# Two feature tiles of the first token chunk side by side, and a last output tile in two halves

## Chip, core and metric

The kernel runs on one core of a Trainium2 chip. The metric is the device time of one launch in microseconds; beside it stands a profile of one execution. TensorE (PE) multiplies, VectorE (DVE) and ScalarE (ACT) move data out of PSUM and split it, GpSimd (POOL) fills constants, and SyncE (SP) issues most DMAs; some stores of the last stage are issued from ScalarE's queue.

## What is computed

Two independent results stand side by side in the output, 2048 x 896 in float32:

```python
def _A_ref(x, dft_seq_re, dft_seq_im, dft_hid_re, dft_hid_im):
    a = jnp.einsum("bsd,ed->bse", x, dft_hid_re)
    b = jnp.einsum("bsd,ed->bse", x, dft_hid_im)
    y = jnp.einsum("ts,bse->bte", dft_seq_re, a) - jnp.einsum("ts,bse->bte", dft_seq_im, b)
    return y

def _B_ref(x, wqkv, wo):
    B, S, D = x.shape          # 1, 2048, 448
    H = 16; Dh = D // H
    qkv = (lambda x, *d: x.transpose(*d))((x @ wqkv).reshape(B, S, 3, H, Dh), 2, 0, 3, 1, 4)
    q, k, v = qkv[0], qkv[1], qkv[2]
    scores = jnp.einsum("bhqd,bhkd->bhqk", q, k) * Dh ** -0.5
    p = _softmax(scores, axis=-1)
    o = jnp.einsum("bhqk,bhkd->bhqd", p, v)
    return (lambda x, *d: x.transpose(*d))(o, 0, 2, 1, 3).reshape(B, S, D) @ wo
```

A is a Fourier mixing of hidden and sequence axis, B attention with 16 heads of 28.

## The kernel before

The tokens of B are cut into four chunks of 512 (`CH`), the columns of query and key weights into seven tiles of 128 (j), the token rows into 16 tiles of 128. Every float32 operand is split into a high part (a copy to fp32r, mostly by ScalarE) and a low part (source less high part, by VectorE); a product is then eleven matmuls (`products`: three k-tiles with high-high, low-high and high-low, and two for the 64 rows that are left). The program has these stages:

- `load_x` loads a chunk of x in four pieces (L573), converts each (L575) and subtracts (L481). `Piece` (by `weights_of`) loads one weight tile (L606), converts it into `whi` (L607) and subtracts it into `wlo` (L611, L620). `load_w` does the same for the value weights, which lie in the tile `wd` (L590, L591, and L481 by the helper `sub`).
- `project(j, w, chunks)` makes tile j of queries and keys for some chunks, eleven matmuls each (L636, by `chain`), copies the bank out (L485 or L487), subtracts the low part (L678) and stores both in DRAM (L681, L682). `values` does the value products (L636 again, with `wd` as the moving operand) and copies them with L711.
- `tops` bounds the scores' maximum from the first keys (matmul L1418, transposition L1421), and its row goes through DRAM (`md`, L1427, L1470) into the query tile.
- `head_once` makes scores (L1434), their exponentials on ScalarE (L1438), and products with the values (L1445) in groups of 16 score tiles. Matmuls of the other stages fill the gaps: first the rest of the projections, then the hidden-axis stage of A (L891), then its sequence-axis stage (L1175), then the output projection (`project_late`: L1669 for three k-tiles, L1700 for the last one).

The order of instructions isn't written by hand. Every operation is a task of `Schedule` with a key (about when it is due), an estimated duration, the tasks that it waits for and the buffers that it takes; a list scheduler walks through time, gives each free engine the ready task of the lowest key, and emits it. So one edit can move instructions on every engine far behind it. On each engine and in each queue what was emitted runs in order. PSUM has eight banks: `fill_s` holds 0 to 3 (all stages but scores), `bank_s` 4 to 7, and it may borrow. `kept` is a pool of 20 buffers of 128 x 2 x 512.

`chain` keeps its matmuls in order among themselves and with all other chains by a shared list:

```python
    last = [None]
...
        last[0] = pe(key + i * d, emit, d=d, deps=[last[0], *more], use=[*use, o, *(then if i == n - 1 else ())])
```

At the start the program warms TensorE with products of the identity (L1528), and asks for chunk 0 of x, the weights of tile 0, the value weights and the other chunks, in this order. In the last stage tiles 8 to 15 of the output have nine of their eleven matmuls in a bank (L1669), the last two are added (L1700), the bank is copied out, and the tile (128 x 448) is stored: odd tiles from ScalarE's queue (L1710), even ones from SP's (L1712). A flag is read by all engines at the end (L1742); it decides on a second way through the program that isn't taken here.

Of the kernel before, what the change touches and what calls it, by code (L numbers as in the profile page):

```python
# [14 lines left out]
AF = mybir.ActivationFunctionType  # L15
# [7 lines left out]
D = 448  # L23
H = 16
DH = 28
P = 128
NT = S // P
CH = 512
NC = S // CH
# [12 lines left out]
QT = NT // NQ  # L42
Q_YO = 2
N_WARM = 11
VALUES = (4, 4, 4, 4)
LEAD = 30.0
LIMIT = 1e36
# [292 lines left out]
def tile_kernel(ctx, tc, xa, wre, wim, wd, xb, wqkv, wo, out):  # L340
# [118 lines left out]
    def pe(key, emit, n=1, d=MS, lat=0.25, **kw):  # L459
        return sch.add({"PE": n * d}, key, emit, lat=lat, **kw)  # L460
# [185 lines left out]
    v_done = {}  # L646
    x_users = []

    def project(j, w, chunks):

        for c in chunks:
            cols = slice(c * CH, (c + 1) * CH)
            o = fill_s.slot()
            xh, xl, x3 = lambda k, cols=cols: lz(x_h, k, cols), lambda k, cols=cols: lz(x_l, k, cols), lambda cols=cols: lz(x_3, cols)
            wh, wl = lambda k: (lambda: w.hi.t[:, k]), lambda k: (lambda: w.lo.t[:, k])
            first = j == 0
            seq = [(b, a) for a, b in products(xh, xl, x3, wh, wl)]
            if first and c == 0:

# [11 lines left out]
            pair = None if st else kept_s.slot()  # L671
            hi, lo = (stage_s.slot(), stage_s.slot()) if st else (Half(pair, 0), Half(pair, 1))
            own = [hi, lo] if st else [pair]
            end = chain(key, seq, o, CH, [], [w.hi, w.lo], M512, own, parts)
            key, out_key = (0.0, 11.0) if first else (key - 10, key - 10)
            as_r, as_f = (lambda t, st=st: t if st else f32r(t)), (lambda t, st=st: f32(t) if st else t)
            a = sch.add({"ACT": ACT_P, "DVE": DVE_P}, key, lambda e, o=o, hi=hi: copy_of(e, as_r(hi.t), o.t), deps=[end], use=[o, *own])
            b = dve(key, lambda o=o, hi=hi, lo=lo: nc.vector.tensor_tensor(  # L678
# [5 lines left out]

    def weights_of(j):
        key = fkey(0, 0) - 12
        return Piece(lambda: wqkv[:, :, j * P:(j + 1) * P], 0.2 if j == 0 else key, "w", j == 0)

    def values(ready, chunks):
        HH = H // 2  # L690
# [837 lines left out]
            nc.tensor.matmul(o.t[:, :P], ident, ident, start=True, stop=True)  # L1528
    pe(-1.0, warm, n=N_WARM, d=0.43, acq=[o])
    load_x(0, 0.1)  # L1530
    w_0 = weights_of(0)
    wv = load_w(w_first, lambda k: wqkv[:, k, 2 * D:], 1.5, early=True)
    for c in range(1, NC):
        load_x(c, 1.0 + 3 * c)
    project(0, w_0, [0])
    values(wv, [0])
    project(0, w_0, [1, 2, 3])
    values(wv, [1, 2, 3])
    x_users.append(v_last[0])
    for j in range(1, 7):  # L1540
        project(j, weights_of(j), range(NC))
    key = fkey(0, 0)
    staged = [d for j in range(1, 5) for c in range(NC) for d in qk_done[j, c]]
    ready = weights_both(key - 11, [v_last[0], *staged])
# [86 lines left out]
    def project_late(w, w_ready):  # L1631
# [29 lines left out]
        for n in range(NT):  # L1661
# [5 lines left out]
            for i, (a, b) in enumerate(seq):  # L1667
                def emit(e, i=i, a=a, b=b, o=o, n=n):
                    nc.tensor.matmul(o.t[:, :D], a(), b(), start=(i == 0), stop=(i == 8 and n < N_HELD))  # L1669
# [23 lines left out]
        for n in range(NT):  # L1693
            c, t = divmod(n, 4)
            key = T_OUT + n
            o = bank_s.slot() if n < N_HELD else held[n][0]

            def emit(e, n=n, o=o, xt=x3[c], t=t):
                for i, y in enumerate((w.h, w.l)):
                    nc.tensor.matmul(o.t[:, :D], xt.t[:, t * P:(t + 1) * P], y[:, 3], start=(i == 0 and n < N_HELD), stop=(i == 1))  # L1700
            p = pe(key, emit, n=2, d=M448, deps=[x3_ready[c], *w_ready, *([] if n < N_HELD else [held[n][1]])], use=[o, x3[c]])
            if n < N_HELD:
                s, at, put = held[n]
                e = dve(key, lambda o=o, at=at: nc.vector.tensor_tensor(at(), at(), o.t[:, :D], op=ALU.add), 0.53, deps=[p, put], use=[o, s])
                dma(key, lambda at=at, n=n: nc.sync.dma_start(out[n * P:(n + 1) * P, D:], at()), deps=[e], use=[s])
            else:
                pair = kept_s.slot()
                e = sch.add({"ACT": 0.43, "DVE": 0.53}, key, lambda e, o=o, pair=pair: copy_of(e, pair.t[:, 0, :D], o.t[:, :D]), deps=[p], use=[o, pair])
                if n % 2:
                    dma_act(key, lambda pair=pair, n=n: nc.scalar.dma_start(out[n * P:(n + 1) * P, D:], pair.t[:, 0, :D]), 3.0, deps=[e], use=[pair])  # L1710
                else:
                    dma(key, lambda pair=pair, n=n: nc.sync.dma_start(out[n * P:(n + 1) * P, D:], pair.t[:, 0, :D]), deps=[e], use=[pair])  # L1712
# [91 lines left out]
```

## Time and profile before

| | us |
|---|---|
| median of three runs | 798.05 |
| lowest and highest of them | 796.93, 800.04 |
| time of the profiled execution | 799.37 |
| its span, first to last instruction | 797.6 |
| TensorE busy in it | 785.1 (98%) |
| ScalarE busy | 598.9 (75%) |
| VectorE busy | 434.4 (54%) |

Times of the trace count from the start of the span. The profiled execution took 1.8 us more than its span, and 1.3 us more than the median. A busy TensorE isn't TensorE at its peak, since a matmul's modelled end lies behind the next one's start; how fast matmuls follow each other is read from their starts. Mean granted clock over the span: 0.994.

### The profile page before, as it was taken

Reading aid. Unit: us, or ns where it says so; the run is one execution under the profiler, and the core shown is the slowest. Engines: PE = TensorE matmul, PEld = TensorE weight load, DVE = VectorE, ACT = ScalarE, POOL = GpSimd, SP = SyncE. Lnnn points to the kernel's source line nnn. Section 1 sums busy time; section 2 is a strip of 40 time slices with the busy share of each in tenths; the row PEclk is TensorE's granted clock in tenths of the full one; section 3 lists DMA queues with packets and bytes.
Section 4 is the critical chain, followed back from the end, with each engine's and each line's share of the span. In section 5 each row is a group of like instructions: output and inputs, shape, how many; then the busy total and the mean of one; then the engine's idle time right before and its main releaser. Section 6 shows DMA issues by size and latency. Waiting matters only on the chain.

```text
span 797.6 us, 14127 instructions
## 1 busy us (share of the span) xinstructions
PE 785.1 (98%) x4721; PEld 476.4 (60%) x4721; DVE 434.4 (54%) x914; ACT 598.9 (75%) x1243; POOL 51.7 (6%) x201
## 2 busy tenths in 40 slices
PE   8999999999999999999999999999999999999997
PEld 7886556576666555555555555555545555555586
DVE  6641443363244363523455986466966968485850
ACT  6106877558778778888888888888888978888941
POOL 3000000000000000000002111011201201101000
PEclk9999999999999999999999999999989999999999
DMA  9657866452584554546459775649848768775642
GB/s 299 213 174 245 222 200 210 135 188 85 155 170 144 165 179 144 152 151 203 131 158 312 240 222 158 219 144 265 264 112 239 231 203 257 254 223 155 184 149 96
DMA packets 138610, 152.58 MB, mean 191 GB/s; under 512 B 31140, under 2 KB 109538, under 8 KB 138530
## 3 DMA queue, kind: packets, MB, share of 16 engines
q1 hardware_dynamic: 137954, 150.69, 61.7%
q8 instruction: 39, 0.64, 0.3%
q10 hardware_dynamic: 576, 0.92, 0.3%
q14 instruction: 41, 0.34, 0.1%
HBM read 110.39 MB, written 50.86 MB: 202 GB/s over the span
## 4 chain that ended last, share of the span: by engine, by line
PE 88%; issue 5%; SPq 2%; DMA 2%; DVE 1%; ACT 1%; POOL 0%; DVEq 0%; POOLq 0%
PE bank L1434 31%; PE bank L1445 27%; PE bank L636 11%; PE bank L1175 10%; PE bank L891 4%; PE bank L1669 4%; PE bank L1700 1%; ACT kept L1438 1%; DMA kept<-wqkv 1%; DMA abd<-kept 1%; PE bank L1418 1%; SPq L1296 1%; PE bank L1518 0%; PE bank L1094 0%; SPq L1297 0%
## 5 line engine op out<-in xcount | busy, mean ns | idle before, releaser
L1438 ACT ACTIVATE kept<-bank 128x512 f32<-128x512 f32 x1024 | 509.8, 669 | 140.6 <-PE bank L1434 135.0
L1434 PE MATMUL bank<-q,k 85*128 85x512 f32 x1024 | 364.1, 424 | 3.3 <-DVE kept L1421 1.3
L1434 PEld LDWEIGHTS bank<-q,k 85*128 85x128 f32 x1024 | 184.3, 190 | 97.2 <-issue 27.4
L1445 PE MATMUL bank<-kept,v 128*32 128x512 f32 x2048 | 234.0, 597 | 0.0
L1445 PEld LDWEIGHTS bank<-kept,v 128*32 128x32 f32 x2048 | 60.1, 110 | 133.8 <-issue 130.3
L1175 PE MATMUL bank<-zt 128*128 128x226 bf16 x448 | 75.1, 265 | 0.0
L487 DVE COPY kept<-bank 128x226 f32<-128x226 f32 (+3 forms) x58 | 27.7, 499 | 81.1 <-PE bank L891 46.8
L636 PE MATMUL bank<-xt,whi 128*128 128x512 f32 x196 | 69.2, 399 | 1.1 <-DVE xt L481 1.1
L1175 PEld LDWEIGHTS <-zt 128*128 128x128 bf16 x448 | 31.0, 99 | 31.0 <-issue 20.6
L636 PEld LDWEIGHTS bank<-xt,whi 128*128 128x128 f32 x196 | 36.7, 190 | 13.2 <-issue 2.5
L1218 DVE TENSOR_TENSOR zt<-wdraw,xraw 128x508 bf16<-128x508 f32 x28 | 19.1, 682 | 45.7 <-PE bank L1175 30.3
L1131 DVE TENSOR_REDUCE diff<-zt 128x1 f32<-128x512 bf16 x66 | 43.5, 672 | 0.9
L636 PE MATMUL bank<-xt,wlo 128*128 128x512 f32 x112 | 43.8, 393 | 0.0
L891 PE MATMUL bank<-wd,whi 128*128 128x450 f32 (+3 forms) x128 | 43.1, 376 | 0.0
L1175 PE MATMUL bank<-xt,whi 128*128 128x448 f32 (+1 forms) x128 | 39.4, 337 | 0.0
L636 PE MATMUL bank<-wd,xt 128*128 128x448 f32 x176 | 37.8, 369 | 0.6 <-DVE wd L481 0.6
L636 PEld LDWEIGHTS bank<-wd,xt 128*128 128x128 f32 x176 | 32.7, 188 | 4.7 <-issue 1.0
L1129 ACT ACTIVATE spent<-zt 128x512 uint8<-128x512 bf16 x46 | 31.6, 686 | 4.0 <-DVE zt L1213 1.9
L485 ACT ACTIVATE kept<-bank 128x448 f32<-128x448 f32 (+5 forms) x21 | 11.7, 588 | 26.4 <-PE bank L1700 13.0
L487 DVE CAST wd<-bank 128x512 fp32r<-128x512 f32 x11 | 7.6, 691 | 40.3 <-PE bank L636 36.9
L1224 POOL TENSOR_TENSOR zt<-wdraw,xraw 128x2 bf16<-128x2 f32 x28 | 9.1, 325 | 302.1 <-DMA wdraw<-wre 143.8
L1421 DVE STREAM_TRANSPOSE kept<-bank 128x512 f32<-128x512 f32 (+1 forms) x20 | 14.2, 711 | 26.0 <-PE bank L1418 25.9
(171 smaller groups left out, 756.4 us busy)
## 6 DMA issues: line engine op xcount, KB each, us to landing
wdraw<-wim SPq DMA_DIRECT2D x38, 256.0 KB
qkd<-wd SPq DMA_DIRECT2D x32, 256.0 KB
wdraw<-wre SPq DMA_DIRECT2D x32, 256.0 KB
q<-qkd SPq DMA_DIRECT2D x64, 112.0 KB
k<-qkd SPq DMA_DIRECT2D x64, 112.0 KB
abd<-kept SPq DMA_DIRECT2D x16, 448.0 KB
kept<-abd SPq DMA_DIRECT2D x16, 448.0 KB
qkd<-kept SPq DMA_DIRECT2D x24, 256.0 KB
```

The costliest lines, as they stand in the source:

```text
L487: nc.vector.tensor_copy(dst, src)
L636: nc.tensor.matmul(o.t[:, :cols], w(), x(), start=(i == 0), stop=(i == n - 1))
L891: nc.tensor.matmul(o.t[:, c0:c1], of(w, i), y(), start=n == 0, stop=n == m)
L1129: nc.scalar.activation(spent, src(), AF.Abs, accum_out=dst)
L1131: nc.vector.tensor_reduce(dst, src(), axis=AX.X, op=ALU.add, apply_absolute_value=True)
L1175: nc.tensor.matmul(o.t[:, at0:at0 + n], cut_of(w.t, e, c), x(), start=first, stop=stop)
L1218: e.tensor_tensor(turned(dl.t, 1, 1, P - 1), mirror(r.t), read(base.t, 1, 1, P - 1), op=minus)
L1421: r = dve(key, lambda o=o, mt=mt: nc.vector.transpose(mt.t[:32 * n, 0], o.t[:32 * n]), 0.64, deps=[m], acq=[mt], use=[o], own=RAW_S)
L1434: m = pe(key, lambda e: nc.tensor.matmul(b.t, KT[h][kt // 4].t[:KR + 1, kt % 4 * P:(kt % 4 + 1) * P], q.t[:KR + 1, :], start=True, stop=True),
L1438: return act(key - 20, lambda: nc.scalar.activation(p.t, b.t, AF.Exp, scale=SCALE), deps=[m], use=[b, pair])
L1445: nc.tensor.matmul(o.t[j * VW:(j + 1) * VW, :], VT[h].t[:, kt // 4, kt % 4, :], tiles[i // 2].t[:, i % 2, :], start=(kt < 4 // len(cs)), s ...
L1669: nc.tensor.matmul(o.t[:, :D], a(), b(), start=(i == 0), stop=(i == 8 and n < N_HELD))
```

## The change

Four edits. The weight tile of j = 1 is loaded early too (`EARLY = 2`), half a unit of key behind that of tile 0, and its chunk 0 is projected right behind that of tile 0; its matmuls there keep an order of their own (a `last` of `[None]`), so that the scheduler may put them between those of tile 0. This chunk of tile 1 goes through a `kept` buffer and not through the staging tiles. Tile 1 then does only chunks 1 to 3 later. In the last stage tile 15 does its last two products in two halves of 224 columns, four matmuls; ScalarE copies the first half and stores it from its own queue, VectorE copies the second and SP stores it. The queues of tiles 8 to 14 are swapped: even ones from ScalarE's, odd ones from SP's.

```diff
--- before.py
+++ after.py
@@ -42,6 +42,8 @@
 QT = NT // NQ
 Q_YO = 2
 N_WARM = 11
+EARLY = 2
+W_STEP = 0.5
 VALUES = (4, 4, 4, 4)
 LEAD = 30.0
 LIMIT = 1e36
@@ -646,14 +648,14 @@
     v_done = {}
     x_users = []
 
-    def project(j, w, chunks):
+    def project(j, w, chunks, last=last):
 
         for c in chunks:
             cols = slice(c * CH, (c + 1) * CH)
             o = fill_s.slot()
             xh, xl, x3 = lambda k, cols=cols: lz(x_h, k, cols), lambda k, cols=cols: lz(x_l, k, cols), lambda cols=cols: lz(x_3, cols)
             wh, wl = lambda k: (lambda: w.hi.t[:, k]), lambda k: (lambda: w.lo.t[:, k])
-            first = j == 0
+            first = j == 0 or j < EARLY and c == 0
             seq = [(b, a) for a, b in products(xh, xl, x3, wh, wl)]
             if first and c == 0:
 
@@ -671,8 +673,8 @@
             pair = None if st else kept_s.slot()
             hi, lo = (stage_s.slot(), stage_s.slot()) if st else (Half(pair, 0), Half(pair, 1))
             own = [hi, lo] if st else [pair]
-            end = chain(key, seq, o, CH, [], [w.hi, w.lo], M512, own, parts)
-            key, out_key = (0.0, 11.0) if first else (key - 10, key - 10)
+            end = chain(key, seq, o, CH, [], [w.hi, w.lo], M512, own, parts, last)
+            key, out_key = (0.0, 11.0 + j) if first else (key - 10, key - 10)
             as_r, as_f = (lambda t, st=st: t if st else f32r(t)), (lambda t, st=st: f32(t) if st else t)
             a = sch.add({"ACT": ACT_P, "DVE": DVE_P}, key, lambda e, o=o, hi=hi: copy_of(e, as_r(hi.t), o.t), deps=[end], use=[o, *own])
             b = dve(key, lambda o=o, hi=hi, lo=lo: nc.vector.tensor_tensor(
@@ -684,7 +686,7 @@
 
     def weights_of(j):
         key = fkey(0, 0) - 12
-        return Piece(lambda: wqkv[:, :, j * P:(j + 1) * P], 0.2 if j == 0 else key, "w", j == 0)
+        return Piece(lambda: wqkv[:, :, j * P:(j + 1) * P], 0.2 + W_STEP * j if j < EARLY else key, "w", j < EARLY)
 
     def values(ready, chunks):
         HH = H // 2
@@ -1528,17 +1530,18 @@
             nc.tensor.matmul(o.t[:, :P], ident, ident, start=True, stop=True)
     pe(-1.0, warm, n=N_WARM, d=0.43, acq=[o])
     load_x(0, 0.1)
-    w_0 = weights_of(0)
+    w_early = [weights_of(j) for j in range(EARLY)]
     wv = load_w(w_first, lambda k: wqkv[:, k, 2 * D:], 1.5, early=True)
     for c in range(1, NC):
         load_x(c, 1.0 + 3 * c)
-    project(0, w_0, [0])
+    for j in range(EARLY):
+        project(j, w_early[j], [0], last if j == 0 else [None])
     values(wv, [0])
-    project(0, w_0, [1, 2, 3])
+    project(0, w_early[0], [1, 2, 3])
     values(wv, [1, 2, 3])
     x_users.append(v_last[0])
     for j in range(1, 7):
-        project(j, weights_of(j), range(NC))
+        project(j, *((w_early[j], range(1, NC)) if j < EARLY else (weights_of(j), range(NC))))
     key = fkey(0, 0)
     staged = [d for j in range(1, 5) for c in range(NC) for d in qk_done[j, c]]
     ready = weights_both(key - 11, [v_last[0], *staged])
@@ -1695,6 +1698,24 @@
             key = T_OUT + n
             o = bank_s.slot() if n < N_HELD else held[n][0]
 
+            if n == NT - 1:
+                pair, half = kept_s.slot(), D // 2
+                for a in range(2):
+                    part = slice(a * half, (a + 1) * half)
+
+                    def emit(e, o=o, xt=x3[c], t=t, part=part, a=a):
+                        for i, y in enumerate((w.h, w.l)):
+                            nc.tensor.matmul(o.t[:, part], xt.t[:, t * P:(t + 1) * P], y[:, 3, part], start=False, stop=(i == 1 and a == 1))
+                    p = pe(key + a / 2, emit, n=2, d=MLOW, deps=[x3_ready[c], *w_ready, held[n][1]], use=[o, x3[c]])
+                    src, to = lambda o=o, part=part: o.t[:, part], lambda pair=pair, part=part: pair.t[:, 0, part]
+                    if a:
+                        e = dve(key, lambda: nc.vector.tensor_copy(to(), src()), 0.32, deps=[p], use=[o, pair])
+                        dma(key, lambda part=part: nc.sync.dma_start(out[n * P:(n + 1) * P, D + half:], to()), 112, deps=[e], use=[pair])
+                    else:
+                        e = act(key, lambda src=src, to=to: nc.scalar.activation(to(), src(), AF.Copy), 0.34, deps=[p], use=[o, pair])
+                        dma_act(key, lambda to=to: nc.scalar.dma_start(out[n * P:(n + 1) * P, D:D + half], to()), 2.5, deps=[e], use=[pair])
+                break
+
             def emit(e, n=n, o=o, xt=x3[c], t=t):
                 for i, y in enumerate((w.h, w.l)):
                     nc.tensor.matmul(o.t[:, :D], xt.t[:, t * P:(t + 1) * P], y[:, 3], start=(i == 0 and n < N_HELD), stop=(i == 1))
@@ -1706,7 +1727,7 @@
             else:
                 pair = kept_s.slot()
                 e = sch.add({"ACT": 0.43, "DVE": 0.53}, key, lambda e, o=o, pair=pair: copy_of(e, pair.t[:, 0, :D], o.t[:, :D]), deps=[p], use=[o, pair])
-                if n % 2:
+                if n % 2 == 0:
                     dma_act(key, lambda pair=pair, n=n: nc.scalar.dma_start(out[n * P:(n + 1) * P, D:], pair.t[:, 0, :D]), 3.0, deps=[e], use=[pair])
                 else:
                     dma(key, lambda pair=pair, n=n: nc.sync.dma_start(out[n * P:(n + 1) * P, D:], pair.t[:, 0, :D]), deps=[e], use=[pair])
```

What this does to the order is seen at three places. First TensorE, from behind the warming products to the first value products; `xt0` is chunk 0 of x, `whi0` and `wlo0` the weights of tile 0, `wd` the value weights. Before:

```order
L636 MATMUL bank0_264<-xt0_193,whi0_201 128x512 x3
L636 MATMUL bank0_264<-xt0_193,wlo0_204 128x512 x2
L636 MATMUL bank0_264<-xt0_193,whi0_201 128x512 x2
L636 MATMUL bank0_264<-xt0_193,wlo0_204 128x512
L636 MATMUL bank0_264<-xt0_193,whi0_201 128x512 x2
L636 MATMUL bank0_264<-xt0_193,wlo0_204 128x512
L636 MATMUL bank1_265<-wd_197,xt0_193 128x448 x9
L636 MATMUL bank2_266<-xt1_194,whi0_201 128x512
L636 MATMUL bank1_265<-wd_197,xt0_193 128x448 x2
L636 MATMUL bank3_267<-wd_197,xt0_193 128x448 x11
```

and after, where `whi1` and `wlo1` are the weights of tile 1 and lines stand two further down:

```order
L638 MATMUL bank0_264<-xt0_193,whi0_201 128x512
L638 MATMUL bank1_265<-xt0_193,whi1_202 128x512 x3
L638 MATMUL bank1_265<-xt0_193,wlo1_205 128x512 x2
L638 MATMUL bank1_265<-xt0_193,whi1_202 128x512
L638 MATMUL bank0_264<-xt0_193,whi0_201 128x512
L638 MATMUL bank0_264<-xt0_193,wlo0_204 128x512
L638 MATMUL bank1_265<-xt0_193,whi1_202 128x512
L638 MATMUL bank1_265<-xt0_193,wlo1_205 128x512
L638 MATMUL bank1_265<-xt0_193,whi1_202 128x512 x2
L638 MATMUL bank1_265<-xt0_193,wlo1_205 128x512
L638 MATMUL bank2_266<-wd_197,xt0_193 128x448 x6
L638 MATMUL bank3_267<-xt1_194,whi0_201 128x512
```

Seven matmuls of tile 1 have come between tile 0's last ones and the value products, and four ahead of them; the first matmul of chunk 1 comes after six value products and not after nine.

Second VectorE in the same stretch, from x's second piece on. Before:

```order
L481 TENSOR_TENSOR xt0_193<-kept1_227,xt0_193 128x512
L481 TENSOR_TENSOR xt0_193<-kept2_228,xt0_193 128x512
L481 TENSOR_TENSOR xt0_193<-kept3_229,xt0_193 64x512
L481 TENSOR_TENSOR wd_197<-kept4_230,wd_197 128x448
L481 TENSOR_TENSOR wd_197<-kept5_231,wd_197 128x448
L481 TENSOR_TENSOR wd_197<-kept6_232,wd_197 128x448
L487 CAST kept2_228<-bank0_264 128x512
L678 TENSOR_TENSOR kept2_228<-bank0_264,kept2_228 128x512
L481 TENSOR_TENSOR wd_197<-kept8_234,wd_197 64x448
```

and after:

```order
L483 TENSOR_TENSOR xt0_193<-kept1_227,xt0_193 128x512
L483 TENSOR_TENSOR xt0_193<-kept2_228,xt0_193 128x512
L613 TENSOR_TENSOR wlo1_205<-wraw1_199,whi1_202 128x384
L622 TENSOR_TENSOR wlo1_205<-wraw1_199,whi1_202 64x128
L483 TENSOR_TENSOR xt0_193<-kept3_229,xt0_193 64x512
L483 TENSOR_TENSOR wd_197<-kept4_230,wd_197 128x448
L483 TENSOR_TENSOR wd_197<-kept6_232,wd_197 128x448
L680 TENSOR_TENSOR kept0_226<-bank0_264,kept0_226 128x512
L489 CAST kept2_228<-bank1_265 128x512
L680 TENSOR_TENSOR kept2_228<-bank1_265,kept2_228 128x512
L483 TENSOR_TENSOR wd_197<-kept7_233,wd_197 128x448
L483 TENSOR_TENSOR wd_197<-kept8_234,wd_197 64x448
```

Two subtractions for the weights of tile 1 stand ahead of x's fourth piece (`kept3`, 64x512), and bank 1's copy and low part ahead of the value weights' third and fourth piece; bank 0's copy (L487 CAST before) has left VectorE. On ScalarE it stands between the second and the third value weight:

```order
L609 ACTIVATE whi1_202<-wraw1_199 128x512
L577 ACTIVATE xt0_193<-kept3_229 128x512
L593 ACTIVATE wd_197<-kept4_230 128x448
L593 ACTIVATE wd_197<-kept6_232 128x448
L487 ACTIVATE kept0_226<-bank0_264 128x512
L593 ACTIVATE wd_197<-kept7_233 128x448
L593 ACTIVATE wd_197<-kept8_234 128x448
L577 ACTIVATE xt1_194<-kept10_236 128x512
```

There the conversion of tile 1's weights has come ahead of x's fourth piece, and bank 0's copy ahead of two value weights.

Third the end of VectorE's list with what each row waits for, the last add of a tile and the copy of the second half:

```order
L1725 TENSOR_TENSOR wdraw_3647<-wdraw_3647,bank6_270 128x448 [waits Activation_49]
L1725 TENSOR_TENSOR wdraw_3647<-wdraw_3647,bank5_269 128x448 [waits Activation_49]
L1725 TENSOR_TENSOR wraw2_200<-wraw2_200,bank0_264 128x448 [waits Activation_49]
L1693 TENSOR_TENSOR q3_219<-kept18_244,q3_219 64x512 [waits DMAHW7_49,Activation_49]
L1712 COPY kept17_243<-bank0_264 128x224 [waits Activation_49]
```

The new copy (L1712) waits for ScalarE (Activation) and for nothing of TensorE's; ScalarE's copy of the first half waits for TensorE. Before, this list ended with the `q3` row.

## Rows read from the trace of the kernel before

**Rows 1.** The page's first lines: span, and busy time of each engine.
```profile
span 797.6 us, 14127 instructions
...
PE 785.1 (98%) x4721; PEld 476.4 (60%) x4721; DVE 434.4 (54%) x914; ACT 598.9 (75%) x1243; POOL 51.7 (6%) x201
```

**Rows 2.** What TensorE waited for: us in total, times, longest.
```profile
PE bank L1434 <- DVE kept L1421: 1.3, 1, 1.3
PE bank L1434 <- DMA q<-md: 1.2, 2, 0.8
...
PE bank L1434 <- DVE wd L678: 0.6, 1, 0.6
```

**Rows 3.** Timeline of TensorE, 5 to 16 us: start, duration, instructions, [idle before].
```profile
10.18 0.50 PE L636 MATMUL bank<-xt,whi 128*128 128x512 f32 x1 [1.05 <-DVE xt L481]
...
10.74 2.01 PE L636 MATMUL bank<-wd,xt 128*128 128x448 f32 x9
12.66 0.50 PE L636 MATMUL bank<-xt,whi 128*128 128x512 f32 x1
13.00 0.36 PE L636 MATMUL bank<-wd,xt 128*128 128x448 f32 x1
13.94 2.30 PE L636 MATMUL bank<-wd,xt 128*128 128x448 f32 x10 [0.58 <-DVE wd L481]
```

**Rows 4.** Timeline of ScalarE, 4 to 15 us.
```profile
7.23 0.63 ACT L575 ACTIVATE xt<-kept 128x512 fp32r<-128x512 f32 x1 [0.66 <-DMA kept<-xb]
8.78 0.63 ACT L575 ACTIVATE xt<-kept 128x512 fp32r<-128x512 f32 x1 [0.92 <-DMA kept<-xb]
...
10.70 1.18 ACT L591 ACTIVATE wd<-kept 128x448 fp32r<-128x448 f32 x2 [0.20 <-DMA kept<-wqkv]
```

**Rows 5.** Timeline of VectorE, 4 to 17 us.
```profile
5.91 0.56 DVE L611 TENSOR_TENSOR wlo<-wraw,whi 128x384 fp32r<-128x384 f32 x1 [0.17 <-ACT whi L607]
6.38 0.28 DVE L620 TENSOR_TENSOR wlo<-wraw,whi 64x128 fp32r<-64x128 f32 x1
...
9.44 0.69 DVE L481 TENSOR_TENSOR xt<-kept,xt 64x512 fp32r<-64x512 f32 x1 [0.86 <-ACT xt L575]
...
11.86 0.68 DVE L487 CAST kept<-bank 128x512 fp32r<-128x512 f32 x1
...
13.18 0.61 DVE L481 TENSOR_TENSOR wd<-kept,wd 64x448 fp32r<-64x448 f32 x1
```

**Rows 6.** Busy time by engine, granted clock, DMA share and GB/s, 10 to 12 us.
```profile
10.00:12.00 2.00, 1.82 (x9) 1.63 (x10) 1.97 (x5) 1.68 (x4) 0.31 (x5) 1.00 1.04 393
```

**Rows 7.** Timeline of TensorE at 21 us, where projections follow each other.
```profile
21.04 0.40 PE L636 MATMUL bank<-xt,whi 128*128 128x512 f32 x1
21.27 0.40 PE L636 MATMUL bank<-xt,wlo 128*128 128x512 f32 x1
```

**Rows 8.** Busy time by engine in windows, columns as in rows 6.
```profile
584.00:586.00 2.00, 2.00 (x5) 0.76 (x5) 1.93 (x5) 2.00 (x5) 0.00 (x0) 1.00 0.23 56
586.00:588.00 2.00, 2.00 (x5) 1.01 (x5) 2.00 (x9) 2.00 (x6) 0.00 (x0) 0.65 0.25 59
588.00:590.00 2.00, 2.00 (x7) 1.67 (x7) 2.00 (x5) 2.00 (x5) 0.00 (x0) 0.50 0.32 114
590.00:595.00 5.00, 5.00 (x32) 1.65 (x35) 2.01 (x4) 3.82 (x10) 0.00 (x0) 0.66 0.76 171
```

**Rows 9.** Timeline of the end, 788 to 798 us.
```profile
791.97 0.54 ACT L485 ACTIVATE kept<-bank 128x448 f32<-128x448 f32 x1 [1.69 <-PE bank L1700]
792.54 0.34 ACTq L1710 DMA_DIRECT2D out<-kept  x1
```

**Rows 10.** ScalarE's groups by line with their shapes: a copy of 224 columns.
```profile
L825 ACT ACTIVATE wd<-kept 128x224 fp32r<-128x224 f32 x2 | 0.8, 400 | 0.0
```

**Rows 11.** VectorE's groups by line with their shapes: a copy of 224 columns.
```profile
L487 DVE COPY kept<-bank 128x224 f32<-128x224 f32 x15 | 5.7, 383 | 0.0
```

## The prediction

> **What bounds the kernel now.** I read the page's first part, then the list of what TensorE waited for, then the timelines of the first 16 us, engine by engine, then the end. The page says that TensorE is busy 98% of the span [rows 1]; the list puts few waits beside it: 3.1 us in three entries, for head loads and evictions [rows 2], and before them 1.6 us for VectorE in the first 14 us [rows 3]. So this is a kernel of TensorE work in program order: an edit gains only what it takes out of a TensorE hole, or what it takes off the last store. The change doesn't take work away. It moves 11 projection matmuls into the hole at the start, moves a weight load with them, and cuts the last tile.
>
> The hole: TensorE has done nine matmuls of chunk 0 when it waits 1.05 us, until 10.18, for the last piece of x, starts the value products, stops again at 12.7, and runs without a break only from 13.94 us, when VectorE has finished the last piece of the value weights (wd) [rows 3]. By then 22 of the 128-column matmuls are done: 11 of the projection, 10 of the value products, one of the next chunk. What is late there is a chain through three parties: the loads, which land one after the other with ScalarE waiting for them [rows 4]; ScalarE's conversions; and VectorE, which subtracts the low halves and must evict bank 0 in between [rows 5]. The DMA engines give 393 GB/s in that stretch at full share [rows 6], so a load more is time more.
>
> **The start, step by step.** (Times of the profile.)
> - *The load.* The second weight tile (256 KB) now goes out ahead of x's fourth piece and the four value weights. Its price has two bounds: the three pieces landing between 8.78 and 10.70 took 0.64 us each, and the one between 7.23 and 8.78 took 1.55 us [rows 4]. 256 KB at 393 GB/s is 0.67 us [rows 6]. I take 0.65: the queue is full by then. So x's fourth piece lands at 9.43, the value weights at 10.07, 10.7, 11.35 and 12.0.
> - *VectorE ahead of x's fourth piece.* The new tile lands at 8.78, ScalarE converts it until 9.41, VectorE subtracts its low part in 0.56 + 0.28 us, a little overlapped, until 10.13 [rows 5]. x's fourth piece (0.69) is then ready at 10.82, where before it was 10.13.
> - *TensorE.* The two last matmuls of bank 0 and the five last of bank 1 follow (7 at 0.23, by the starts of two neighbours [rows 7]): until 12.45. Six value products at 0.205 (nine start and end in 2.01 us, the last of them 0.37 long [rows 3]): until 13.7; all they need was ready by 12.0.
> - *Evictions.* ScalarE now copies bank 0 (the order shows it between the second and third value weight): 11.5 to 12.1; ScalarE then converts the third and fourth value weight until 12.7 and 13.3, x1's first piece until 13.93. VectorE takes bank 0's low part 12.1 to 12.8, bank 1's copy and low part until 14.15 (some 0.69 each [rows 5]), then the value weights at 0.6 each: 14.75 and 15.36. Add the 0.15 us that stood between VectorE's end at 13.79 and TensorE's 13.94 [rows 3, 5]: TensorE runs without a break from 15.50.
> - *Sum.* It starts 1.56 us later, with 33 matmuls done in place of 22: 11 x 0.229 = 2.52 us ahead. Net **-0.96 us**. The same delay comes out of VectorE's bill alone: 0.84 + 1.37 of new work, 0.68 gone to ScalarE, 1.53. Bounds: with VectorE's new work hidden, only the load delays (0.65), -1.87 us; with the load at 1.55 and VectorE's 0.9 behind it as in the sum, -0.06.
>
> Behind it I see no new hole at once: 34 value products (7.0 us) and the other 32 projections of tile 0 (7.3 us) are next in TensorE's order, and VectorE gets to the x chunks that they need in time. Chunk 0's stores now go out between x3's first and second piece (two 256 KB stores, 1.3 us on the SP queue's transfers), but x3 isn't needed until some 27 us.
>
> **The middle.** The planner lays everything out anew for some 300 us: at the 25th group of score-times-value matmuls the two orders have done the same work to one matmul, and from the 31st on they are alike to the matmul. The work is the same: 484 projection matmuls, 256 of the hidden stage, 1024 scores. It matters only which waits change. TensorE waited 1.2 us for the row of maxima (q<-md) before the scores got going, and 1.3 and 0.6 for evictions further on [rows 2]. Counted in the two programs' orders, 263 and 287 projection matmuls now stand ahead of the first use of the third and fourth query tile, where it was 236 and 257. 27 x 0.229 = 6.2 us of cover, less the 0.96: if the loads come no later, the 1.2 us go. But the loads of that chain are laid out anew too. I take half, **-0.6 us**; the bounds are -3.1 (all three waits gone) and +3.1 (as much again).
>
> The gain is carried to the end only if nothing further on is tied to something else. The weakest place is 575 to 595 us: few filler matmuls, ScalarE and VectorE full, and the granted clock falls to 0.65, 0.50 and 0.66 in three windows [rows 8]. The order there is the same before and after. A VectorE whose work itself follows from TensorE's progress shifts with it, so I let the gain pass.
>
> **The end.** Before, ScalarE copies the last tile in 0.54 us from 791.97 and its DMA issue ends at 792.88; the span ends 4.7 us later [rows 9]. After, four matmuls of 224 columns take what two of 448 took. The price of the halves isn't in this trace as such: ScalarE took 0.40 for 128x224 elsewhere and VectorE 0.38 [rows 10, 11]. Overlapped, ScalarE would start 0.2 earlier and both issues would be out by 792.7, 0.2 us earlier than before. In series (VectorE's copy behind ScalarE's, as the awaited semaphore in the order's row says) the second issue ends at 791.97 + 0.40 + 0.03 + 0.38 + 0.03 + 0.34 = 793.15, 0.27 later. Half of 224 KB less per queue is 0.29 us at 393 GB/s. I take the series: **0.0 us**, bounds -0.5 and +0.3. Swapping the two store queues among the tiles before costs nothing: the next tile's matmuls (2.2 us) hide each store.
>
> The Trainium skill bears on it: PSUM — Partial Sum Buffer, section "PSUM bank collisions raise a hardware error", says that two engines must not touch one bank in the same quadrant at once, even in disjoint columns, and two readers neither. By it the halves have to go in series, which is the sum above; without it the end would give 0.2 to 0.5 us. No row of this trace tests it.
>
> **Sum.** -0.96 - 0.6 + 0.0 = -1.6 us on the profiled execution's 799.37 us: 797.8. That execution lies 1.3 us above the median of the three runs shown (798.05; they go from 796.93 to 800.04). From the median: **796.5 us**. 0.5% is 4.0 us, about what a measurement of this kernel can tell from no change; so the likeliest answer is "not to be told apart", with a small gain in it.
>
> **Rivals.**
> 1. *More is gained.* The start is load-bound only (-1.87), the waits for maxima and one of the evictions go (-1.8), the halves overlap (-0.3): 794.1 us. For it: VectorE still had waits of its own before 10 us. Against: from 10 to 12 us it was busy 1.97 of 2 us [rows 6].
> 2. *The gain is swallowed.* Either new waits in the re-laid head loads take it back, or the stretch at 575 to 595 us is held by VectorE, ScalarE or transfers that don't come earlier: 798.0. For it: VectorE 2.00 of 2 us there [rows 8]. Against: its work there is made of what TensorE finished before.
> 3. *Slower: the start loses.* TensorE takes its matmuls in order, so the second tile's seven stand before the value products. If the load costs 1.55 and VectorE's 2.21 us of new work is paid in full behind it, the unbroken run begins at 13.94 + 3.76 = 17.7: 1.24 us lost, 799.3. It decides at 16.46 us (13.94 + 2.52): later than that, the change loses.
> 4. *The clock.* The three windows lost 0.35 x 2 + 0.5 x 2 + 0.34 x 5 = 3.4 us of clock [rows 8], after a stretch in which TensorE issued 5 matmuls in 2 us. A second such stretch gives 799.9, its absence 793.1. Against: the order there hasn't changed.
>
> **How the numbers follow.** The forecast 0.50, rival 1 0.15, rival 2 0.18, rival 3 0.11, rival 4 0.06 (half each way). The forecast's own spread is 795.2 to 797.8 (start between its bounds, runs). For 8 in 10 I reach to rival 1 and past rival 2 to rival 3: 794.2 to 799.4. Faster by over 0.5% needs 794.06 or less: half of rival 1 and a part of rival 4, 0.09. Slower by over 0.5% needs 802.0: only bound cases of the middle, 0.04. The rest, 0.87, within.
>
> **What the profile of the changed kernel would show.** The start is right if VectorE subtracts the fourth value weight at about 15 us and TensorE's unbroken run begins between 14.6 and 16.4 with 33 matmuls behind it; wrong in size if it begins before 14.6, wrong in sign after 16.5. The middle is right if TensorE's wait for q<-md is under 0.7 us. The end is right if VectorE's 224-column copy starts only after ScalarE's. The forecast fails if TensorE shows a wait of several us that the list of before doesn't have, or another count of half-clock windows.

## The result, and the profile after

| | before | after |
|---|---|---|
| median of 21 runs each, us | 798.05 | 800.52 |
| lowest, highest | 796.03, 801.15 | 797.88, 805.78 |
| profiled execution, its span | 799.37, 797.6 | 800.69, 798.9 |

The ratio is 1.0033, interval 1.0022 to 1.0044: 1.8 to 3.5 us slower, 2.6 in the middle. That is within 0.5%, as the likeliest class had it, but on the wrong side, and the 800.52 lie above the range's 799.4.

The first lines of the page, against [rows 1]: as much TensorE work, 1.3 us more span.

```profile
span 798.9 us, 14127 instructions
...
PE 784.8 (98%) x4723; PEld 477.0 (60%) x4723; DVE 432.9 (54%) x911; ACT 599.2 (75%) x1247; POOL 52.1 (7%) x201
```

**The start went as forecast.** The timelines of TensorE and of VectorE, against [rows 3, 5]:

```profile
7.61 0.50 PE L638 MATMUL bank<-xt,whi 128*128 128x512 f32 x1 [1.20 <-ACT xt L577]
...
12.39 1.38 PE L638 MATMUL bank<-wd,xt 128*128 128x448 f32 x6
...
14.68 7.54 PE L638 MATMUL bank<-wd,xt 128*128 128x448 f32 x35 [0.22 <-DVE wd L483]
```

```profile
13.40 0.69 DVE L680 TENSOR_TENSOR kept<-bank,kept 128x512 fp32r<-128x512 f32 x1
14.01 1.14 DVE L483 TENSOR_TENSOR wd<-kept,wd 128x448 fp32r<-128x448 f32 x2
```

The unbroken run begins at 14.68 us with 31 matmuls done, behind an idle time of 0.22; before it began at 13.94 with 22. 0.74 later and 9 x 0.229 ahead is -1.3 us. The six value products end at 13.77 (13.7 in the working).

**The middle lost.** What TensorE waited for, against [rows 2]: the waits for `q<-md`, for the eviction L1421 and for L678 are off the list, and a new one heads it. Where the wait for L1421 stood, behind the matmul of the twelfth `qb` load, TensorE now waits 1.0 us for another transposition on VectorE (L1502).

```profile
PE bank L1420 <- DMA qb<-qkd: 1.9, 1, 1.9
...
PE bank L1436 <- DVE kept L1502: 1.0, 1, 1.0
```

TensorE's timeline shows the place, and the windows the clock (columns as in [rows 6]):

```profile
243.74 0.47 PE L1420 MATMUL bank<-qb,kb 112*128 112x512 f32 x1 [1.95 <-DMA qb<-qkd]
244.14 5.31 PE L1447 MATMUL bank<-kept,v 128*32 128x512 f32 x32
```

```profile
238.00:240.00 2.00, 2.00 (x11) 1.46 (x10) 1.00 (x5) 2.00 (x6) 0.00 (x0) 1.00 0.87 6
...
242.00:244.00 2.00, 0.26 (x1) 0.19 (x1) 0.36 (x1) 1.50 (x4) 0.00 (x0) 1.00 0.96 285
244.00:246.00 2.00, 2.00 (x13) 0.55 (x16) 1.76 (x4) 0.00 (x0) 0.00 (x0) 0.54 0.84 257
246.00:248.00 2.00, 2.00 (x20) 0.38 (x16) 0.32 (x2) 0.00 (x0) 0.00 (x0) 0.61 0.53 165
```

After 1.95 us without work the granted clock falls to about half (0.54 and 0.61 in two windows), and 32 matmuls that take 3.64 us at full clock take 5.31. Why is `qb` late? SP's queue says it:

```profile
235.81 3.60 SPq L1033 DMA_DIRECT2D edge<-wre  x3
239.50 1.19 SPq L1417 DMA_DIRECT2D qb<-qkd  x1
```

Three loads of one column each of `wre` (128x16x1, single 4-byte elements) go out just ahead of it. They keep SP for 3.60 us and the DMA engines 87% busy at 6 GB/s (window 238 to 240). In the old order two of them stood ahead of this load, one behind, and TensorE, which used it at 242.54 us, had no wait there:

```profile
223.56 2.54 SPq L1031 DMA_DIRECT2D edge<-wre  x2
226.19 1.44 SPq L1415 DMA_DIRECT2D qb<-qkd  x1
227.68 0.56 SPq L1031 DMA_DIRECT2D edge<-wre  x1
```

The queue is one part of it. There is a single `qb` buffer (`NQB = 1`), so this load goes out only behind the matmul that reads the load before. That matmul stood at 223.27 us in the old order, 19.3 us ahead of the next, and stands at 235.53 in the new one, 8.2 us ahead. Of these 8.2 us the edge loads took 3.6.

**The end lost too.** The last rows, against [rows 9 to 11]:

```profile
791.74 0.36 ACT L1715 ACTIVATE kept<-bank 128x224 f32<-128x224 f32 x1 [1.72 <-PE bank L1708]
792.13 0.34 ACTq L1716 DMA_DIRECT2D out<-kept  x1
792.13 0.39 DVE L1712 COPY kept<-bank 128x224 f32<-128x224 f32 x1 [16.34 <-ACT kept L1715]
792.55 0.33 SPq L1713 DMA_DIRECT2D out<-kept  x1
```

The halves go in series, with about the durations that the working used (0.36 and 0.39 us). But the span ends 7.2 us after ScalarE's last copy begins (798.9 less 791.74), and before it was 5.6 (797.6 less 791.97). The trace's records of SP behind its last transfer: reading the flag from 792.94, register operations, the branch at 793.84, and nothing more until 796.99, 3.15 us later. By then both stores had landed; SP passes eight waits in 0.6 us. Before, SP had branched at 791.62, was back at 794.15, and waited until 795.84 for ScalarE's store: SP's way lay beneath that transfer.

### The profile page after: what moved, and what is told of

Its sections match the earlier page's. It is cut to its first block, busy times and chain, and to the rows that moved or that the text cites. A ratio compares the mean times of both kernels' runs of the same rounds, so it can differ in the third digit from the quotient of the medians.

```text
span 798.9 us, 14127 instructions
## 1 busy us (share of the span) xinstructions
PE 784.8 (98%) x4723; PEld 477.0 (60%) x4723; DVE 432.9 (54%) x911; ACT 599.2 (75%) x1247; POOL 52.1 (7%) x201
## 4 chain that ended last, share of the span: by engine, by line
PE 95%; DMA 2%; ACT 1%; DVE 1%; issue 0%; SPq 0%; POOL 0%; POOLq 0%; ACTq 0%
PE bank L1436 32%; PE bank L1447 28%; PE bank L638 13%; PE bank L1177 10%; PE bank L893 5%; PE bank L1672 4%; PE bank L1420 1%; PE bank L1721 1%; DMA kept<-xb 1%; ACT kept L1440 1%; DMA xraw<-basd 1%; DMA qb<-qkd 1%; PE bank L1520 0%; PE bank L1096 0%; ACT xt L577 0%; PE bank L1191 0%
## 5 line engine op out<-in xcount | busy, mean ns | idle before, releaser
L489 DVE COPY kept<-bank 128x446 f32<-128x446 f32 (+3 forms) x56 | 27.0, 503 | 71.4 <-PE bank L893 55.5
L487 ACT ACTIVATE kept<-bank 128x448 f32<-128x448 f32 (+5 forms) x23 | 12.6, 574 | 22.6 <-PE bank L1721 11.3
L489 DVE CAST kept<-bank 128x512 fp32r<-128x512 f32 x9 | 6.2, 690 | 40.8 <-PE bank L638 40.7
L1502 DVE STREAM_TRANSPOSE kept<-bank 128x512 f32<-128x512 f32 (+1 forms) x19 | 13.5, 712 | 26.3 <-PE bank L1447 18.5
```

The source lines that it names most:

```text
L489: nc.vector.tensor_copy(dst, src)
L1502: t = dve(key - 20, lambda: nc.vector.transpose(pair.t[:m, 0], o.t[:m]), 0.66, deps=[dep], use=[o, pair], own=RAW_S)
```

## The experiments

**Theory 1:** the start wins about what was forecast; the new order in the middle loses it again by `qb` behind the edge loads, and by the clock that falls after that wait; the new end makes SP the last to store, so that its flag, branch and return (4.1 us from the flag's reading on) stand at the end of the program. **Rivals:** the early tile itself loses; the halves cost; the wait is chance; the 4-byte transfers are in the way from any queue; the clock falls for another reason. All times are against the kernel before on the same chip; the ratios are turned into us with 798.

**1. The start alone** (start_only). The last stage as before, the rest as after.

```diff
-            if n == NT - 1:
...
-                if n % 2 == 0:
+                if n % 2:
```

> Tile 1 early, the old end of the program (tile 15 whole, stored from ScalarE's queue; odd tiles from ScalarE's, even ones from SP's). TensorE's order is that of the changed kernel up to the last tile. Theory 1 (the middle gives back what the start wins, and the slowdown sits in the end): the wait for qb near 243.7 us and the half-clock stretch behind it come again, TensorE's last work ends 0 to 0.5 us earlier than before, and the time is that of before, -0.8 to +0.3 us. Rival (the start with its re-laid middle is what loses, and the end is innocent): +1.5 to +3 us, like the whole change. Rival (the wait for qb is a matter of one execution): no such wait, -2 to -3.5 us.

Measured: 1.0023 (1.0007 to 1.0038), +1.8 us. The wait for `qb` was there again (1.9 us), the clock 0.50 and 0.68 in the same two windows. So the wait belongs to the order, not to one execution; and by the ratio start and middle together lose by themselves, more than theory 1 allowed and as the rival had it. Where these 1.8 us lie its profile can't show: the profiled execution, of 798.18 us, is next to the shortest of the twelve.

**2. The end alone** (tail_only), on the kernel before. TensorE's order is that of before up to tile 15.

> The kernel before with the new end alone: tile 15 in two halves, the second copied by VectorE and stored by SP, queues of tiles 8 to 14 swapped. TensorE's order up to the last tile is that of before. Theory 1: SP's last transfer now stands where SP was idle, its reading of the flag, its branch and the 3 us until it is seen again come after it, and the span ends 7.1 us behind TensorE's last matmul in place of 5.6: +1.2 to +1.8 us. Rival (the end costs nothing; the loss is the middle's): -0.3 to +0.4 us.

**3. Only the queues swapped** (parity_only), tile 15 whole:

```diff
-                if n % 2:
+                if n % 2 == 0:
```

> The kernel before with only the queues of tiles 8 to 15 swapped; tile 15 is copied whole and stored whole by SP. Theory 1 (SP being the last to store is what costs): SP's transfer is issued at about 792.9, its flag, branch and return follow, and the time is +0.9 to +1.7 us, no halves needed. Rival (the halves cost: two serial copies and four matmuls in place of two): 0 to +0.3 us. Rival (VectorE's late copy, and with it its late branch, costs): 0.

**4. The end alone, both halves stored from ScalarE's queue** (tail_act_queue; the edit is against tail_only):

```diff
-                        dma(key, lambda part=part: nc.sync.dma_start(out[n * P:(n + 1) * P, D + half:], to()), 112, deps=[e], use=[pair])
+                        dma_act(key, lambda part=part: nc.scalar.dma_start(out[n * P:(n + 1) * P, D + half:], to()), 2.5, deps=[e], use=[pair])
```

> The new end, but the second half too is stored from ScalarE's queue; VectorE still copies it. Theory 1: SP is done before 791 us as before, so what is left is the serial copies, +0.1 to +0.5 us. Rival (it is VectorE's late branch, seen again 3.7 us after it in the changed kernel): +1 us or more stays, as with the new end whole. Rival (the halves themselves): the same as with the new end whole.

Measured, in the order of 2 to 4: +0.9 us (-0.6 to +2.3), +1.0 (-0.3 to +2.4) and -0.2 (-1.4 to +1.0). The times alone don't part these, since single executions of one kernel differ by several us; the span behind the last copy does better, because it varies less, by 1.2 us with the old end and by 0.2 with the halves:

| end of the program | last copy starts to span's end, us |
|---|---|
| whole tile, ScalarE's queue (before, start_only, start_edge_pool, before_edge_pool, start_edge_act, start_fill_wait, start_w_step_03) | 5.6, 5.1, 6.0, 5.6, 6.0, 5.6, 6.3 |
| halves, the second from SP's (after, tail_only, after_edge_pool) | 7.2, 7.2, 7.0 |
| whole tile, SP's queue (parity_only) | 6.4 |
| halves, both from ScalarE's queue (tail_act_queue) | 5.7 |

By the means the new end costs 7.1 - 5.7 = 1.4 us. With SP out of it (5.7) the halves can't be told from the old end, and VectorE's late copy, which is in tail_act_queue too, costs nothing that shows. A whole tile stored by SP (6.4) lies just above the old end's range, in one execution: that half of theory 1 is a hint here and not shown. The records point the same way: SP was back from its branch 4.5 us after the last copy's start there and 4.9 to 5.3 with the halves, where in before the last store was seen landed after 3.9.

**5. No branch** (before_no_branch, tail_only_no_branch). Both ends once more, without the flag, the branch and the second way through the program, which these two leave out:

```diff
-    again = nc.values_load(flag, min_val=0, max_val=1)
-    with tc.If(again != 0):
...
```

> The kernel before without the reading of the flag, the branch on it and the second way through the program, which this leaves out. Theory 1 (with ScalarE storing last, SP's own branch is hidden under that store's landing, and ScalarE's comes after its issue): the span ends some 4.5 to 5 us behind the start of ScalarE's last copy in place of 5.1 to 6.0, 0.5 to 1 us less.

> The kernel before with the new end, and without the flag, the branch and the second way, which this leaves out. Theory 1 (what the new end costs is SP's flag, branch and return, 3.9 to 4.4 us behind its last transfer, longer than the transfer's landing): the span ends 4.7 to 5.5 us behind the start of ScalarE's last copy in place of 7.0 to 7.2, and no more than 0.5 us later than the old end without the branch. Rival (the halves or a late transfer of SP cost by themselves): the difference of 1.5 us between new and old end stays.

The last copy and what follows, first of the old end without the branch (span 795.0 us), then of the new (797.4):

```profile
791.46 0.54 ACT L485 ACTIVATE kept<-bank 128x448 f32<-128x448 f32 x1 [1.69 <-PE bank L1700]
792.03 0.34 ACTq L1710 DMA_DIRECT2D out<-kept  x1
```

```profile
793.85 0.36 ACT L1712 ACTIVATE kept<-bank 128x224 f32<-128x224 f32 x1 [1.71 <-PE bank L1705]
...
794.66 0.33 SPq L1710 DMA_DIRECT2D out<-kept  x1
```

From the last copy to the end it is 3.5 us in both (795.0 - 791.46, 797.4 - 793.85): the difference between the ends is gone, with halves, VectorE's copy and SP's late transfer all in place. So it was the flag, the branch and the return from it. The times: 0.9985 (0.9962 to 1.0007) and 0.9983 (0.9962 to 1.0003).

The old end was expected to lose 0.5 to 1 us of tail and lost 2.1, more than theory 1 said. ScalarE's own branch isn't the reason: in before ScalarE was back at 796.26, while SP went on passing its waits until 796.7. By SP's records the last store was seen landed 3.3 us after its issue began (792.54 to 795.84), without the branch after 2.0 (792.03 to 794.02); from there to the end it took 1.7 and 1.0 us. The pages also list DMA packets of a kind called instruction, of 8 and 16 KB. First before, then before_no_branch:

```profile
q8 instruction: 39, 0.64, 0.3%
...
q14 instruction: 41, 0.34, 0.1%
```

```profile
q8 instruction: 37, 0.61, 0.3%
q14 instruction: 35, 0.29, 0.1%
```

The eight that are missing without the branch are two on q8 and six on q14; before has six such packets from 790.16 us to its end, the kernels without the branch none in their last 9 us. That the store and the returns wait for them fits, but no run shows it.

**6. The edge loads out of SP's queue.** No matmul changes its place. On the start alone, once from GpSimd's queue (start_edge_pool), once from ScalarE's (start_edge_act); then, GpSimd's, on the whole change (after_edge_pool) and on the kernel before (before_edge_pool):

```diff
-        edge_ready[part] = [dma(key + 20 + i, lambda i=i: nc.sync.dma_start(
+        edge_ready[part] = [dma(key + 20 + i, lambda i=i: (nc.sync if part else nc.gpsimd).dma_start(
```

> Tile 1 early, old end, and the three strided edge loads (128x16x1, L1033) that stand ahead of the qb load in SP's queue go out from GpSimd's queue; no instruction of TensorE changes its place. Theory 1 (the edge loads ahead of qb in SP's queue make the wait at 243.7 us, and the wait is followed by the half-clock stretch): qb is issued at about 236 us and not at 239.5, no wait for qb, granted clock 1.00 at 244 to 248 us, TensorE's excess over its own pitch from 240 to 250 us under 1 us in place of 4.4, and the time 3 to 4 us under that of the same kernel without this edit: 1.2 to 2.2 us under before. Rival (the 4-byte transfers hold the DMA engines, whichever queue they come from): the wait stays above 1 us, and the time within 1 us of the kernel without this edit. Rival (the half-clock stretch comes from the order of work at 244 us, not from the wait): wait gone, clock still about 0.5, 2 us under it.

> The same, with the three edge loads issued from ScalarE's queue, a queue without descriptors made by GpSimd. Theory 1: as with GpSimd's queue, less at most the 3 x 0.34 us that ScalarE gives to issuing them. Rival (the transfers themselves hold the DMA engines): the wait for qb stays above 1 us.

> The whole change (new end too) with the edge loads from GpSimd's queue. Theory 1: the middle's 3.9 us come back, the end's 1.5 to 1.8 us stay: 3 to 4 us under the changed kernel, 0.3 to 1.3 us under before, and 1.3 to 1.9 us over the kernel with the old end and the same edit.

> The kernel before with its edge loads from GpSimd's queue: the control for the edit itself. There two of the edge loads stand ahead of qb and one behind, and TensorE has no wait there. Theory 1: the edit is worth nothing by itself, -0.5 to +0.3 us. Rival (the strided loads cost something wherever they are): -1 us or more.

With GpSimd's queue: 0.9964 (0.9939 to 0.9990), **2.9 us under before** by the ratio (0.8 to 4.9; the plain medians, 797.39 and 798.33, lie 0.9 apart), and 4.7 under the same kernel without the edit, which ran on another chip. TensorE's timeline and a window:

```profile
241.06 0.47 PE L1420 MATMUL bank<-qb,kb 112*128 112x512 f32 x1 [0.50 <-DMA qb<-qkd]
241.46 3.64 PE L1447 MATMUL bank<-kept,v 128*32 128x512 f32 x32
```

```profile
242.00:244.00 2.00, 2.00 (x24) 0.56 (x20) 1.64 (x5) 0.29 (x1) 0.00 (x0) 1.00 0.55 140
```

The wait is 0.50 in place of 1.95, the clock stays at 1.00, the 32 matmuls take 3.64. Two things changed with the queue. GpSimd was free, so the loads left at 225.2 to 227.6 us, ten us before SP would have issued them. And their packets are others: on GpSimd's queue (q0) the three loads are 144 packets of up to 256 bytes, on ScalarE's (q10) 6192 of 4 bytes beside the 576 packets of the stores. The pages of start_edge_pool and start_edge_act:

```profile
q0 software_dynamic: 144, 0.02, 0.3%
```

```profile
q10 hardware_dynamic: 6768, 0.94, 0.7%
```

The control on the kernel before gave 0.9993 (0.9964 to 1.0023), nothing to be told from 1. The whole change with this edit: 0.9986 (0.9958 to 1.0014); its end took 7.0 us again, and its one profiled execution had another wait for `qb`, of 2.33 us, at 125 us.

From ScalarE's queue the time went up: 1.0043 (1.0015 to 1.0071). The loads left between 232.2 and 236.2 us there, and TensorE stood:

```profile
242.54 1.22 PE L1436 MATMUL bank<-q,k 85*128 85x512 f32 x2 [4.68 <-ACT kept L1440]
```

```profile
234.00:236.00 2.00, 2.00 (x21) 0.42 (x13) 0.00 (x0) 0.36 (x1) 0.00 (x0) 1.00 0.63 4
236.00:238.00 2.00, 1.86 (x12) 1.24 (x8) 1.39 (x2) 0.00 (x0) 0.00 (x0) 1.00 0.74 6
```

The DMA engines are 63 to 74% busy with 4 to 6 GB/s; ScalarE meanwhile idled 7.5 us for a query store (`qkd`). SP's records say why that store was late: a load ahead of it (`basd`, L940), which shares a semaphore with the first edge load, waited 5.2 us until that had landed, and the stores left only at 236.69 and 237.42 us. So that rival is right in part: as 4-byte packets these loads hold up what is due while they run, from SP's queue and from ScalarE's. Which of the two helped on GpSimd's queue, the early time or the fewer packets, no run parts.

**7. The wait filled with work** (start_fill_wait). Nine products of the identity ahead of the matmul that waits for `qb`:

```diff
+                for _ in range(9 if (g, c) == (2, 1) else 0):
+                    nc.tensor.matmul(o.t[:, :P], ident, ident, start=True, stop=True)
```

> Tile 1 early, old end, and nine products of the identity (128x128, into the bank that the next matmul overwrites) ahead of the one matmul that waits for qb at 243.7 us; by the 0.213 us at which such products of four passes follow each other in the profile they take 1.9 us, as long as the wait. Nothing else changes its place. Theory 1 (the idle time of the wait is what the clock falls after): granted clock 1.00 at 244 to 248, the group of score-times-value matmuls behind it takes 3.6 us and not 5.3, and the time is 1.7 us under the kernel without the nine products. Rival (the clock falls for another reason there, the loads or the order of work): clock 0.5 again, time within 0.5 us of it.

```profile
240.76 2.25 PE L1422 MATMUL bank<-ident 128*128 128x128 f32 x18
243.22 0.50 PE L1423 MATMUL bank<-qb,kb 112*128 112x512 f32 x1 [0.20 <-DMA qb<-qkd]
243.65 3.64 PE L1451 MATMUL bank<-kept,v 128*32 128x512 f32 x32
```

`qb` is as late as before, and the 32 matmuls take 3.64 us: what lowered the clock there is the idle time. The time fell from +1.8 to -0.2 us (0.9998, 0.9983 to 1.0013), with products that nobody needs.

**8. Another draw of the planner** (start_w_step_03).

```diff
-W_STEP = 0.5
+W_STEP = 0.3
```

> Tile 1 early, old end, W_STEP = 0.3 in place of 0.5: tile 1's weights are loaded one piece earlier (ahead of x's third piece), and the planner lays out the middle in another way, in which the qb load of the second group of heads goes out ahead of all four edge loads. Theory 1 (the middle's loss is a matter of this one order, not of the early tile): no wait of over 1 us for qb between 220 and 260 us and no half-clock stretch there; the start keeps its 0.8 to 1.3 us; the time is 1 to 3 us under before. Rival (the early tile itself loses in the middle): at or over before.

At 240 us it did as expected, but where 1 to 3 us less had been expected the kernel took **21.5 us more**: 1.0269 (1.0245 to 1.0294). The list of TensorE's waits:

```profile
PE bank L1672 <- DVE kept L1275: 5.9, 1, 5.9
PE bank L1672 <- ACT wdraw L487: 2.6, 5, 0.6
```

This order reaches the output projection with the sequence stage of A not yet evicted: TensorE stands 5.9 us until 766.83 and has granted clocks of 0.50 to 0.82 in the six windows from 764 to 776. A key that moved one load by one piece in the first 8 us decided what 770 us look like.

## Why the prediction was wrong

The wrong steps are **The end** and **The middle**. The table sums, for each matmul, the time to the next one's start less the pitch at which such matmuls follow each other (0.229 us for 512 columns, and so on): what TensorE lost, in us. Worked out from the starts in the trace.

| stretch, us | old order, mean of 6 profiles | after | start_only | start_edge_pool |
|---|---|---|---|---|
| 0 to 20 | 3.2 (2.7 to 4.2) | 2.0 | 2.5 | 1.4 |
| 20 to 230 | 8.7 (8.0 to 9.7) | 8.2 | 7.7 | 7.4 |
| 230 to 260 | 1.5 (1.3 to 1.8) | 6.0 | 6.0 | 3.3 |
| 260 to 560 | 20.6 (19.4 to 22.6) | 18.8 | 18.6 | 19.0 |
| 560 on | 22.3 (21.6 to 22.9) | 21.2 | 20.9 | 22.7 |

- **The start: right.** -0.96 forecast; the three new-order kernels of the table lie 0.7 to 1.8 us under the mean of six, 1.2 on average. The run began at 14.68, inside the forecast's 14.6 to 16.4 but 0.8 us before its middle, with 31 matmuls done and not 33: VectorE ended the fourth value weight at 15.15 (15.36 in the working), and TensorE had to wait for the third alone. In the other five profiles of this order it began between 14.07 and 15.23. The working had no wait for x's second or third piece; here TensorE waited 1.20 us at 7.61, and of these profiles start_edge_pool's alone has no such wait. By the order's rows five of tile 1's matmuls stand behind tile 0's last two, and six ahead of them; the seven that the text and rival 3 name are these five and the two.
- **The middle: the half that was counted came, the other was not looked for.** Until 230 us the waits for maxima went (-0.5 to -1.3, forecast -0.6; the old order's own profiles lie 1.7 apart there). Then 4.5 us were lost at once, more than the upper bound (+3.1). That bound priced "as much again" of old waits. What failed was to read the new order at SP's queue: it showed the `qb` load behind three edge loads, and the trace of before showed what these cost (2.54 us for two), but the text compared matmuls only, and so didn't see that one `qb` buffer now had 8.2 us between two uses and not 19.3. And a wait was counted at its own length, though 1.95 us of it drew 1.7 us of half clock behind it. Rival 2 and rival 4 described the two parts, but neither put them together.
- **Carried to the end: not refuted.** The half-clock stretch at 580 to 595 us [rows 8] is in every profile of either order, and not longer in the new one; only start_w_step_03, whose order is a third one, lacks it.
- **The end: right in every duration, wrong in the sum.** 0.0 forecast, bounds -0.5 and +0.3; 1.4 measured (1.5 between the profiles of before and after). The sum ended at the second store's issue (+0.27 in the text) and took what follows an issue to be the same on each engine. It isn't: behind SP's stand 4.1 us of flag, branch and return, which had been hidden. The sentence on swapped queues spoke of the tiles before the last, where nothing refutes it; for the last tile the text priced copies and bytes and gave the change of the last storing engine no price at all. The halves' order in series followed from the awaited semaphore; the rule of the Trainium skill cited for it (PSUM — Partial Sum Buffer, "PSUM bank collisions raise a hardware error") was not put to a test by any run.

For the whole change the rows give -1.2 - 0.5 + 4.5 - 1.8 - 1.1 and +1.4 for the end, +1.3 us, as the two spans do (1.3); the ratio says 2.6 (1.8 to 3.5). For start_only the same rows add up to -0.6 us, its ratio to +1.8 (0.6 to 3.0). What lies between is no more than single executions of one kernel differ by, and wasn't settled, so the traces place only a part of the loss; nor was the -1.8 from 260 to 560 us, where the old order's wait of 1.3 us for an eviction [rows 2] has a counterpart of 0.8 to 1.3 us in the table's new ones. Open is also what makes the return from the branch take 3 us; only that it goes with the branch was shown.

## What to carry to other kernels

Where a scheduler lays a program out anew, compare the DMA queues of old and new order at each load that TensorE waits for, not only the matmuls: one load behind three slow ones cost more than the whole start had won, and giving the slow ones an idle queue, which sent them early and in fewer packets, turned +1.8 us into -2.9 by the ratios. Before moving the last store to another engine, look at what that engine still has to do after it. Price a wait of TensorE of about two us with the clock that follows it, and time an innocent neighbouring setting too, before crediting an edit with what may be the planner's draw.

## What was not expected of the hardware

- A wait of 1.95 us cost nearly twice its length here, 1.95 and 1.7 us. Granted clocks of 0.50 to 0.67 also followed 1.52 us of idle TensorE (at 284.3 us, tail_only), 2.33 us (at 125 us, after_edge_pool) and 4.68 us (start_edge_act); the clock stayed at 1.00 after 0.50 and after 1.27 (until 286.65 us, before), and when the 1.95 were filled with products. The wait's length alone doesn't decide: 1.38 us in start_fill_wait (until 292.93) were followed by 0.73 and 0.50, 1.48 in before_no_branch (until 285.96) by 1.00. Executions of one order differ by this too: TensorE's wait behind the matmul of the twelfth `qb` load took 0.8 to 1.5 us in the seven profiles of the old order, and two of them had the half clock after it.
- SP, ScalarE and VectorE, branching over a part of the program that isn't taken, show their next record some 3 us later: SP 2.5 us before and 3.15 after, ScalarE 2.8 (793.47 to 796.26) and 3.6 (793.06 to 796.69), VectorE 3.2 before (775.86 to 779.04). GpSimd took 0.2 (770.20 to 770.38).
- Loads of single 4-byte elements kept the DMA engines 63 to 87% busy at 4 to 6 GB/s, where 393 GB/s were seen at full share [rows 6]. The same three loads are 6192 packets from ScalarE's queue and 144 from GpSimd's.
